# Short convolution and routed experts on one core: earlier halo loads, wider spacing of the expert batches, a bank of their own for the expert outputs, and counts summed in PSUM

## The chip, the cores and the metric

The kernel runs on one core of one Trainium2 chip. The metric is the device time of one execution in microseconds, as the median of several. The engines are called PE (TensorE, matmuls; PEld is its loading of weights), DVE (VectorE), ACT (ScalarE), POOL (GpSimd) and SP (SyncE, which here only issues DMAs). "SPq" or "POOLq" is the instruction sequencer of an engine.

## The reference

The input x has 8 sequences of 4160 rows with 192 numbers each. Each row is first replaced by a weighted sum of itself and the six rows before it, with seven softmax weights for each of eight heads of 24 numbers:

```
w = exp(weight_gen - max) ; w = w / (sum(w) + 1e-9)          # (B, S, 8 heads, 7 taps)
out[b, s, h, :] = sum over k of w[b, s, h, k] * x_pad[b, s + k, h, :]   # six zero rows ahead of each sequence
```

On that result, called y here, a gate picks 128 rows of every sequence, and only these go through a two-layer expert:

```
scores = y @ w_gate                                          # (B, S)
top_idx = the 128 rows of each sequence with the highest score
out[top_idx] = y[top_idx] + sigmoid(scores) * (relu(y[top_idx] @ w1) @ w2)   # 192 -> 1024 -> 192
```

All other rows of the output are y itself.

## The kernel before

**Layout.** The 33,280 rows are dealt to 128 partitions, 260 consecutive rows each, 16 partitions per sequence. Each partition needs the six rows ahead of its first row, the *halo*; for the first partition of a sequence they are zeros. x is read in chunks as float16 into a ring of `RING` = 168 row places (`xr`), by DMAs on POOL's queue (the type is changed on the way). A chunk is asked for when the ACT copy of a certain group of transposes begins, so POOL's loads follow the scoring, not the clock.

**Conv.** The loop runs over g = 0 to 65, four rows of every partition at a time, and each g has two halves. `products` (line 791) multiplies the seven shifted windows of x by the weights on DVE into a float16 tile (three tiles, `prodp`). `tap_sums` (line 801) adds the seven taps on PE with an identity matrix into a PSUM tile `cps`, one g later. `store` (line 809) copies it on ACT into one of three tiles `co`, and SP sends that to the output in two DMAs (line 811). A product covers all seven taps in one instruction (5376 numbers per partition) until the scores are complete; from then on, at g = 46, it is split in four and three taps, one part in each half (3072 and 2304 numbers).

**Weights.** weight_gen comes in 18 pieces on SP's queue (`load_wg`). For each, ACT makes the exponentials (line 643), PE sums the taps into the PSUM bank "den" (line 189), ACT turns the sum into its inverse by a logarithm and an exponential (lines 197 and 199), DVE multiplies (line 658), and ACT writes each weight twice (`dup_weights`, line 772) in the form that the products read.

**Scores.** They are found from x and not from y: `dots` transposes x on PE (line 719), ACT copies the transposes out (line 723), and PE multiplies them by a small matrix `gmat` that holds the gate vector, head by head (line 704, PSUM bank "yps"). `score` combines these with the weights. `gmat` is built on POOL with `affine_select` from four small loads of the gate vector (lines 106 to 119); those loads stand on SP's queue between the first piece of weights and the halo.

**The order of the work is written out by hand.** Every half of every g emits its product, then lets each of several generators do one step (`advance`), then emits the tap sums. A generator's step ends at `yield`. All engines therefore run their queues in this written order, and a wait of one instruction holds all that stands behind it on its engine. One advance of the generator `sel` happens per half once all scores are there, that is from g = 46: 40 advances while the conv loop lasts. After it, the `while` loop at line 917 goes on advancing `sel`, and after each advance emits the scatters that are ready.

**Selection** (`threshold_selection`). Each partition finds its 40 highest scores in five rounds of top 8. Four rounds then narrow a threshold for each sequence: DVE compares the 40 values with 23 thresholds (`above`, line 492, 920 results), sums the 40 results of each threshold (`cnt`, line 498), PE adds these over the 16 partitions of a sequence (`tot`, line 501), and DVE reads `tot` to move the threshold (lines 506 to 518). Then the row numbers are packed and a flag tells whether the list was too short; in that case a slow path after the loop does everything again. The value is read by all engines at line 929, after the loop.

**Experts** (`expert_pass`). For each of the eight sequences there is one batch of 128 rows. POOL gathers weights and windows of x by row number (lines 249 and 271). Ten steps follow, and the dictionary `steps` says how many advances after the start of its batch each is made; batches start `EVERY` = 3 advances apart, the first one `GWAIT` = 4 advances after the gathers were asked for:

```
0: row_weights, 1: scale_weights, 2: double, 3: tap_rows, 4: conv_rows,
5: turn_rows, 6: lambda b: hidden(b, 0), 7: lambda b: hidden(b, 1),
8: outputs, 9: hand_over,
```

`row_weights`: exponentials, tap sums and inverse on ACT, PE, ACT. `scale_weights`: two DVE products (lines 304 and 308). `double`: each weight written twice by ACT (`wes`, line 314). `tap_rows`: products of seven taps on DVE (line 320). `conv_rows`: tap sums on PE (`aps`, line 335) and two ACT copies. `turn_rows`: two transposes on PE (`tp`, line 347) and an ACT copy. `hidden`: half of the first layer on PE and a relu on ACT (line 369), twice. `outputs`: the second layer on PE (`yep`, line 377). `hand_over`: DVE scales by the gate value and adds the row (line 385). Inside one advance the steps of older batches come first. Of the eight PSUM banks, `cps` takes four, the transposes and the hidden layer share two ("tps"), and two single ones are "yps" and "den". Tap sums, `tp` and `yep` use "den"; `aps` and the selection's small results use "yps".

**End.** `scatter_rows` (line 417) writes the 128 rows of a batch over the conv's result, by an indirect DMA on POOL. It must come after all conv stores.

Of the kernel before, what the change touches and what calls it, by code (L numbers as in the profile page):

```python
# [20 lines left out]
def kernel(  # L21
# [22 lines left out]

    RING = 168
    C = 4
# [28 lines left out]

    nc.scalar.preload_act_table_set("natural_log_exp_and_others")

    scores = scp.tile([P, SP], FP32)
# [21 lines left out]

    wcol = scp.tile([P, 3], FP32)
    scrap = scp.tile([1, 1], FP32)

    def load_gate():
        wgv = moe_w_gate.rearrange("(d o) -> d o", o=1)
        nc.sync.dma_start(out=wcol[:, 0:1], in_=wgv[0:128, :])
        nc.sync.dma_start(out=wcol[0:64, 1:2], in_=wgv[128:192, :])
        nc.sync.dma_start(out=wcol[64:128, 1:2], in_=wgv[0:64, :])
        nc.sync.dma_start(out=wcol[:, 2:3], in_=wgv[64:192, :])

    def gate_matrix():
        gsel = scp.tile([P, 4, H], FP32)
        for j, (col, off) in enumerate(((0, 0), (1, 128), (1, -64), (2, 64))):
            nc.gpsimd.affine_select(
                out=gsel[:, j, :], in_=wcol[:, col:col + 1].to_broadcast([P, H]),
                pattern=[[-G, H]], compare_op=ALU.is_ge, fill=0.0,
                base=off, channel_multiplier=1,
            )
            nc.gpsimd.affine_select(
                out=gmat[:, j, :], in_=gsel[:, j, :],  # L120
                pattern=[[G, H]], compare_op=ALU.is_ge, fill=0.0,
                base=G - 1 - off, channel_multiplier=-1,
            )

    def selection_masks():
        nc.gpsimd.memset(ones32[:, :], 1.0)
# [75 lines left out]
    def expert_pass(rowf, gates, result, big):  # L202
# [92 lines left out]

        def row_weights(b):
            nc.scalar.activation(
                out=es[:, b, :, :],
                in_=wsel[:, b, :].rearrange("p (h k) -> p k h", k=K), func=AF.Exp
            )  # L300
            rws[b] = inverse(tap_sum(lambda k: es[:, b:b + 1, k, :], 1, H), 1, H)

# [28 lines left out]
        def conv_rows(b):  # L331
            mp = mp_of(b)
            aps = ps1.tile([P, D], FP32, tag="yps", name="aps")
            for k in range(K):
# [39 lines left out]
        def outputs(b):  # L374
            yep = ps1.tile([P, D], FP32, tag="den", name="yep")
            for j in range(FC):
# [15 lines left out]
        def hand_over(b):  # L392
# [3 lines left out]

        steps = {
            0: row_weights, 1: scale_weights, 2: double, 3: tap_rows, 4: conv_rows,
            5: turn_rows, 6: lambda b: hidden(b, 0), 7: lambda b: hidden(b, 1),
            8: outputs, 9: hand_over,  # L400
        }
        for _ in range(GWAIT):
            yield
        for t in range(EVERY * (B - 1) + 10):
            for off in sorted(steps, reverse=True):
# [29 lines left out]
    def threshold_selection():  # L435
# [49 lines left out]
        for r in range(ROUNDS):  # L485
# [18 lines left out]
            ge = scp.tile([P, NTHR], FP32, tag="ge", name="ge")  # L504
            nge = scp.tile([P, 1], FP32, tag="nge", name="nge")
            nc.vector.tensor_scalar(
                out=ge[:, :], in0=tot[:, :], scalar1=float(CAP) - 0.5, scalar2=None,
                op0=ALU.is_ge,
# [75 lines left out]
    def phase():  # L584
# [222 lines left out]
        def store(s, cps):  # L807
            co = outp.tile([P, 2, HB], FP32, tag="co", name="co")
            nc.scalar.copy(out=co[:, :, :], in_=cps[:, :, 0:HB])  # L809
            for j in range(2):  # L810
# [6 lines left out]
                )  # L817

        def selected():
            yield from threshold_selection()  # L820
# [5 lines left out]

        load_x(0, 4)
        load_wg(0)
        load_gate()
        make_identity(nc, identity[:])  # L830
        nc.vector.tensor_copy(out=ident16[:, :], in_=identity[:, :])
        halo = prodp.tile([P, PAD * D], FP32, tag="prod", name="halo")
        nc.vector.memset(halo[0:1, :], 0.0)
        for p0, p1 in ((1, Q), (Q, P)):
            nc.sync.dma_start(
                out=halo[p0:p1, :],
# [3 lines left out]
                ),  # L840
            )
        load_wg(1)
        load_x(4, 12)
        gate_matrix()
        selection_masks()
        load_wg(2)
        start_p = scp.tile([P, 1], FP32)
# [8 lines left out]
        for n in range(2):  # L856
# [3 lines left out]
            dup_weights(n)  # L860
            if n == 0:
                nc.vector.tensor_scalar(
                    out=xflat[:, 0:PAD * D], in0=halo[:, :],
# [12 lines left out]
        for g in range(NSUB + 1):  # L876
# [3 lines left out]
            for half in range(2):  # L880
# [28 lines left out]
            if g > 0:  # L909
                store(g - 1, cps)  # L910
            if g == 10:
                selection_constants()
# [16 lines left out]
    flag_v = nc.values_load(fast["flag"][0:1, 0:1], min_val=0, max_val=2 * P * B)  # L929
    with tc.If(flag_v > 0):  # L930
        with ExitStack() as fctx:
# [81 lines left out]
```

The softmax here doesn't subtract the row's maximum and nothing guards it: scores larger than these inputs give would overflow.

## Time and profile before

| | us |
|---|---|
| time, median of 3 (lowest, highest) | 317.03 (315.77, 319.07) |
| span of the profiled execution | 312.6 |
| DVE busy | 249.6 (80%) |
| PE busy | 194.0 (62%) |
| ACT busy | 188.9 (60%) |
| POOL busy | 56.5 (18%) |
| first conv product begins | 15.0 |
| first top-8 search (selection) begins | 182.9 |
| last eviction of a conv result begins | 288.3 |
| last scatter begins | 303.3 |

The page gives busy time over the whole span, and the kernel has stages with different limits, so the shares say little alone. Useful are the same numbers in stretches of the span, the list of who waited for whom, and the timeline around one step. A wait counts where its engine sets the pace of that stretch; the same wait on an engine with slack costs nothing.

### The profile page before, as it was taken

The page shows a single profiled execution, that of the slowest core. Times are in us where ns is not written, and L with a number is a line of the kernel's source. Part 1 is how long each engine was busy: PE and PEld are TensorE (multiplying, and loading weights), DVE is VectorE, ACT ScalarE, POOL GpSimd, SP SyncE. Part 2 cuts the span into 40 slices and gives each one's busy share as a digit, 9 for nine tenths or more (in the row PEclk, how much of TensorE's full clock was granted, in tenths as well). Part 3 has the DMA queues.
Part 4 walks back from the last instruction along what each step waited for, and adds up shares of the span by engine and source line. Part 5 has one row for each costly group of instructions (what it writes and reads, how often), then busy time and mean ns, then how long its engine had stood idle before and what let it go on. Part 6 is the DMA issues. An engine that isn't in the chain of part 4 may idle for free.

```text
span 312.6 us, 7490 instructions
## 1 busy us (share of the span) xinstructions
PE 194.0 (62%) x3177; PEld 123.2 (39%) x3177; DVE 249.6 (80%) x249; ACT 188.9 (60%) x282; POOL 56.5 (18%) x89
## 2 busy tenths in 40 slices
PE   0049778968697969698884850315727777778100
PEld 0026445635465636465552420103314454545000
DVE  2298995999989998999799999999997788882000
ACT  3279997899989979889684321111615557555100
POOL 3500000101010200101400000000348870000270
PEclk9999895989989779799799575555857999999755
DMA  7797999999999997999996331112467986233220
GB/s 96 221 242 226 219 249 241 193 240 271 260 256 228 257 253 150 214 216 206 229 221 181 102 103 51 50 42 60 74 183 122 175 195 145 55 100 101 72 77 13
DMA packets 29233, 51.50 MB, mean 165 GB/s; under 512 B 4933, under 2 KB 22603, under 8 KB 29194
## 3 DMA queue, kind: packets, MB, share of 16 engines
q0 software_dynamic: 7232, 17.34, 35.1%
q1 hardware_dynamic: 21962, 33.62, 34.3%
q8 instruction: 27, 0.44, 0.6%
q14 instruction: 12, 0.10, 0.1%
HBM read 41.60 MB, written 26.35 MB: 217 GB/s over the span
## 4 chain that ended last, share of the span: by engine, by line
DVE 27%; ACT 23%; PE 18%; DMA 17%; issue 8%; POOL 3%; SPq 2%; POOLq 0%; ACTq 0%; DVEq 0%
DVE prod L791 16%; DMA out_dram<-co 14%; PE cps L801 8%; ACT co L809 6%; ACT xT L723 5%; ACT e L643 4%; PE tps L719 3%; ACT wd L772 3%; DMA wg_t<-in_weight_gen_dram 3%; POOL out_dram L417 2%; PE den L189 2%; DVE above L492 1%; PE yps L704 1%; DVE cnt L498 1%; PE sps L750 1%
## 5 line engine op out<-in xcount | busy, mean ns | idle before, releaser
L791 DVE TENSOR_TENSOR prod<-xr,wd 128x5376 f16<-128x5376 f16 (+1 forms) x84 | 192.5, 2317 | 9.3 <-PE cps L801 5.5
L801 PE MATMUL cps<-prod,ident 64*64 64x384 f16 x1820 | 112.0, 375 | 9.0 <-DVE prod L791 8.9
L809 ACT COPY co<-cps 128x768 f32<-128x768 f32 x65 | 52.5, 808 | 47.8 <-PE cps L801 33.0
L801 PEld LDWEIGHTS <-ident 64*64 64x64 f16 x1820 | 49.9, 119 | 61.5 <-issue 26.4
L723 ACT COPY xT<-tps 128x1024 f16<-128x1024 f16 (+1 forms) x50 | 50.7, 1021 | 8.0 <-PE tps L719 7.7
L601 POOL DMA_DIRECT2D xr<-in_x_dram x28 | 15.1, 539 | 122.8 <-ACT xT L723 103.4
L719 PE MATMUL tps<-ident,xr 128*128 128x128 f16 x399 | 34.5, 236 | 2.4 <-DMA xr<-in_x_dram 2.4
L643 ACT ACTIVATE e<-wg_t 128x896 f16<-128x896 f32 (+2 forms) x18 | 30.0, 1666 | 8.0 <-DMA wg_t<-in_weight_gen_dram 8.0
L772 ACT COPY wd<-w 128x1792 f16<-128x1792 f16 (+2 forms) x18 | 28.0, 1554 | 0.8 <-DVE w L658 0.8
L189 PEld LDWEIGHTS <-ident 128*128 128x128 f16 x182 | 10.6, 104 | 43.3 <-issue 40.3
L719 PEld LDWEIGHTS <-xr 128*128 128x128 f16 x399 | 25.8, 105 | 2.9 <-DMA xr<-in_x_dram 2.6
L189 PE MATMUL den<-e,ident 128*128 128x128 f16 (+2 forms) x126 | 10.9, 235 | 24.2 <-ACT e L643 19.4
L704 PEld LDWEIGHTS <-xT 128*128 128x128 f16 x399 | 14.4, 98 | 23.8 <-issue 17.7
L704 PE MATMUL yps<-gmat,xT 128*128 128x8 f16 (+1 forms) x399 | 17.9, 169 | 9.0 <-ACT y L709 7.0
L249 POOL DMA_INDIRECT wsel<-in_weight_gen_dram,row_i x8 | 10.3, 1288 | 70.0 <-DVE win_i L217 67.9
L271 POOL DMA_INDIRECT xr<-in_x_dram,win_i x8 | 14.0, 1754 | 3.7 <-DVE xr L320 1.6
L417 POOL DMA_INDIRECT out_dram<-xr,row_i x8 | 7.8, 979 | 37.9 <-issue 37.9
L750 PE MATMUL sps<-sp,ident 128*128 128x256 f16 (+2 forms) x63 | 8.9, 290 | 7.8 <-ACT lnd L197 7.3
L501 PE MATMUL tot<-cnt,block 128*128 128x23 f16 x4 | 0.7, 178 | 19.1 <-DVE cnt L498 19.1
L369 ACT ACTIVATE hT<-hps 128x512 bf16<-128x512 f32 x16 | 9.5, 601 | 5.0 <-PE hps L365 5.0
L320 DVE TENSOR_TENSOR xr<-xr,wes 128x1344 f16<-128x1344 f16 x8 | 6.9, 857 | 6.8 <-ACT wes L314 6.8
L658 DVE TENSOR_TENSOR w<-e,r 128x896 f16<-128x896 f16 (+2 forms) x18 | 10.3, 572 | 2.2 <-ACT r L199 2.1
(126 smaller groups left out, 167.1 us busy)
## 6 DMA issues: line engine op xcount, KB each, us to landing
out_dram<-co SPq DMA_DIRECT2D x130, 192.0 KB, 5.2
xr<-in_x_dram POOLq DMA_DIRECT2D x22, 480.0 KB, 8.0
wg_t<-in_weight_gen_dram SPq DMA_DIRECT2D x15, 448.0 KB, 6.4
xr<-in_x_dram POOLq DMA_DIRECT2D x2, 576.0 KB, 8.0
halo<-in_x_dram SPq DMA_DIRECT2D x1, 504.0 KB
wg_t<-in_weight_gen_dram SPq DMA_DIRECT2D x2, 224.0 KB, 8.0
xr<-in_x_dram POOLq DMA_DIRECT2D x1, 384.0 KB, 7.0
w_sb<-in_moe_w_dram POOLq DMA_DIRECT2D x1, 384.0 KB
```

The lines of the kernel that those rows point to most:

```text
L189: nc.tensor.matmul(out=den[:, :, :], lhsT=ident16[:, :], rhs=e_k(k), start=(k == 0), stop=(k == K - 1),)
L271: nc.gpsimd.indirect_dma_start(out=win_of(b), out_offset=None, in_=x_elems, in_offset=bass.IndirectOffsetOnAxis(ap=win_i[:, b:b + 1], axis=0),
L417: ins = nc.gpsimd.indirect_dma_start(out=out_flat[:, :], out_offset=bass.IndirectOffsetOnAxis(ap=result["at"][:, b:b + 1], axis=0), in_=re ...
L601: return nc.gpsimd.dma_start(out=xr[:, o:o + b - a, :], in_=bass.AP(tensor=x_flat.tensor, offset=x_flat.offset + a * D, ap=[[SP * D, P], [ ...
L643: begun = nc.scalar.activation(out=es[n][:, :, :, :], in_=wgts[n].rearrange("p (s c) h k -> p s k (c h)", c=C), func=AF.Exp)
L704: nc.tensor.matmul(out=o, lhsT=lhs, rhs=m, start=(w == 0), stop=(w == 2), skip_group_check=True,)
L719: nc.tensor.transpose(out=tps[:, j, :], in_=xflat[:, e0:e0 + RUN], identity=ident16[:, :],)
L723: begun = nc.scalar.copy(out=xT[:, 0:m, :], in_=tps[:, 0:m, :])
L772: nc.scalar.copy(out=wd[:, 0:b - a, :, :, :], in_=w16[:, a:b, :, :, None].to_broadcast([P, b - a, K, CH, 2]),)
L791: nc.vector.tensor_tensor(out=pv[:, k0:k1], in0=xwin[:, k0:k1], in1=wv[:, k0:k1], op=MUL)
L801: nc.tensor.matmul(out=cps[64 * j:64 * j + 64, i, 0:HB], lhsT=ident16[rows, rows], rhs=pf[rows, k, j * HB:(j + 1) * HB], start=(k == 0), s ...
L809: nc.scalar.copy(out=co[:, :, :], in_=cps[:, :, 0:HB])
```

## The change

It has five parts.

1. *Start.* The two halo loads become the first instructions of ACT's queue, ahead of ACT's table load, and the larger one goes first. The four small loads of the gate vector move to ACT's queue, behind the first duplicated weights. The masks of the gate matrix are then made on POOL without the vector (`gate_masks`), and DVE multiplies the vector in after g = 1. The first three weight pieces stand together on SP's queue. This is to let the first product have its data earlier.
2. *Space.* The ring of x is shortened from 168 to 160 rows, and the room goes to a fourth `co` tile, so that an eviction need not wait for a store that is still under way.
3. *Counts.* The DVE sum over 40 results is gone. Five matmuls of 23 x 8 columns add the results over partitions and over five groups of the 40 in PSUM, and DVE sums the remaining 8.
4. *Spacing and bank.* `row_weights` is cut in two steps, the steps stand partly two advances apart, a batch lasts 13 advances and not 10, and batches start every 4 advances and not 3. The first starts one advance earlier. The last batches so come to lie past the conv loop. `yep` has the bank "yps", `aps` moves to "den". This is to take hand-overs between engines out of the way of the products.
5. *Flag.* All engines read the flag at g = 61 in the loop.

The diff, cut to its core:

```diff
-    RING = 168
+    RING = 160
...
-    nc.scalar.preload_act_table_set("natural_log_exp_and_others")
...
     def load_gate():
...
-        nc.sync.dma_start(out=wcol[:, 0:1], in_=wgv[0:128, :])
+        nc.scalar.dma_start(out=wcol[:, 0:1], in_=wgv[0:128, :])
...
+    def gate_matrix():
+        for j, (col, _) in enumerate(GATE_RUNS):
+            nc.vector.tensor_scalar(
+                out=gmat[:, j, :], in0=gsel[:, j, :], scalar1=wcol[:, col:col + 1],
+                scalar2=None, op0=MUL,
+            )
...
-        def row_weights(b):
+        def row_exps(b):
             nc.scalar.activation(
...
+        def row_sums(b):
             rws[b] = inverse(tap_sum(lambda k: es[:, b:b + 1, k, :], 1, H), 1, H)
...
-            aps = ps1.tile([P, D], FP32, tag="yps", name="aps")
+            aps = ps1.tile([P, D], FP32, tag="den", name="aps")
...
-            yep = ps1.tile([P, D], FP32, tag="den", name="yep")
+            yep = ps1.tile([P, D], FP32, tag="yps", name="yep")
...
-            0: row_weights, 1: scale_weights, 2: double, 3: tap_rows, 4: conv_rows,
-            5: turn_rows, 6: lambda b: hidden(b, 0), 7: lambda b: hidden(b, 1),
-            8: outputs, 9: hand_over,
+            0: row_exps, 1: row_sums, 3: scale_weights, 4: double, 6: tap_rows,
+            7: conv_rows, 8: turn_rows, 9: lambda b: hidden(b, 0),
+            10: lambda b: hidden(b, 1), 11: outputs, 12: hand_over,
...
-            above = scp.tile([P, NTHR, NLIST], BF16, tag="above", name="above")
+            above = scp.tile([P, NTHR, NLIST], FP16, tag="above", name="above")
...
-            cnt = scp.tile([P, NTHR], FP16, tag="cnt", name="cnt")
-            with nc.allow_low_precision("small counts are exact in fp16"):
-                nc.vector.tensor_reduce(out=cnt[:, :], in_=above[:, :, :], axis=AX.X, op=ADD)
             yield
-            tot = ps1.tile([P, NTHR], FP32, tag="yps", name="tot")
-            nc.tensor.matmul(
-                out=tot[:, :], lhsT=block16[:, :], rhs=cnt[:, :], start=True, stop=True
-            )
+            tot = ps1.tile([P, NTHR, 8], FP32, tag="yps", name="tot")
+            for c in range(0, NLIST, 8):
+                nc.tensor.matmul(
+                    out=tot[:, :, :], lhsT=block16[:, :], rhs=above[:, :, c:c + 8],
+                    start=(c == 0), stop=(c == NLIST - 8),
+                )
+            cnt = scp.tile([P, NTHR], FP32, tag="cnt", name="cnt")
+            nc.vector.tensor_reduce(out=cnt[:, :], in_=tot[:, :, :], axis=AX.X, op=ADD)
...
-        outp = cctx.enter_context(tc.tile_pool(name="outp", bufs=3))
+        outp = cctx.enter_context(tc.tile_pool(name="outp", bufs=4))
...
-        load_x(0, 4)
-        load_wg(0)
-        load_gate()
...
-        for p0, p1 in ((1, Q), (Q, P)):
-            nc.sync.dma_start(
+        for p0, p1 in ((Q, P), (1, Q)):
+            nc.scalar.dma_start(
                 out=halo[p0:p1, :],
...
+        nc.scalar.preload_act_table_set("natural_log_exp_and_others")
+        load_wg(0)
+        load_x(0, 4)
...
             if n == 0:
+                load_gate()
...
+                    if half == 1 and g == NSUB - 4:
+                        read_flag()
...
-    GWAIT = 4
-    EVERY = 3
+    GWAIT = 3
+    EVERY = 4
```

More of the change, by code (lines that the diff above doesn't have):

```diff
@@ L101 @@
     wcol = scp.tile([P, 3], FP32)
+    gsel = scp.tile([P, 4, H], FP32)
     scrap = scp.tile([1, 1], FP32)
@@ L105, in load_gate, with gate_masks @@
         wgv = moe_w_gate.rearrange("(d o) -> d o", o=1)
-        nc.sync.dma_start(out=wcol[:, 0:1], in_=wgv[0:128, :])
[L107 to L113, printed above, removed]
+        nc.scalar.dma_start(out=wcol[:, 0:1], in_=wgv[0:128, :])
+        nc.scalar.dma_start(out=wcol[0:64, 1:2], in_=wgv[128:192, :])
+        nc.scalar.dma_start(out=wcol[64:128, 1:2], in_=wgv[0:64, :])
+        nc.scalar.dma_start(out=wcol[:, 2:3], in_=wgv[64:192, :])
+    GATE_RUNS = ((0, 0), (1, 128), (1, -64), (2, 64))
+    def gate_masks():
+        nc.gpsimd.memset(ones32[:, :], 1.0)
+        for j, (_, off) in enumerate(GATE_RUNS):
             nc.gpsimd.affine_select(
-                out=gsel[:, j, :], in_=wcol[:, col:col + 1].to_broadcast([P, H]),
+                out=gsel[:, j, :], in_=ones32[:, 0:H],
                 pattern=[[-G, H]], compare_op=ALU.is_ge, fill=0.0,
@@ L119, in gate_matrix @@
             nc.gpsimd.affine_select(
-                out=gmat[:, j, :], in_=gsel[:, j, :],
+                out=gsel[:, j, :], in_=gsel[:, j, :],
                 pattern=[[G, H]], compare_op=ALU.is_ge, fill=0.0,
@@ L123, in gate_matrix @@
             )
+    def gate_matrix():
[4 more added lines that the diff above has]
+            )
     def selection_masks():
-        nc.gpsimd.memset(ones32[:, :], 1.0)
         bo = blockones.rearrange("p (b q) -> p b q", q=Q)
@@ L403, in expert_pass @@
             yield
-        for t in range(EVERY * (B - 1) + 10):
+        for t in range(EVERY * (B - 1) + max(steps) + 1):
             for off in sorted(steps, reverse=True):
@@ L506, in threshold_selection @@
             nc.vector.tensor_scalar(
-                out=ge[:, :], in0=tot[:, :], scalar1=float(CAP) - 0.5, scalar2=None,
+                out=ge[:, :], in0=cnt[:, :], scalar1=float(CAP) - 0.5, scalar2=None,
                 op0=ALU.is_ge,
@@ L817, in store, with read_flag @@
                 )
+        def read_flag():
+            fast["raised"] = nc.values_load(
+                fast["flag"][0:1, 0:1], min_val=0, max_val=2 * P * B
+            )
         def selected():
@@ L825, in selected @@
             fast["complete"] = True
-        load_x(0, 4)
-        load_wg(0)
-        load_gate()
-        make_identity(nc, identity[:])
-        nc.vector.tensor_copy(out=ident16[:, :], in_=identity[:, :])
         halo = prodp.tile([P, PAD * D], FP32, tag="prod", name="halo")
-        nc.vector.memset(halo[0:1, :], 0.0)
-        for p0, p1 in ((1, Q), (Q, P)):
-            nc.sync.dma_start(
+        for p0, p1 in ((Q, P), (1, Q)):
+            nc.scalar.dma_start(
                 out=halo[p0:p1, :],
@@ L841, in phase @@
             )
+        nc.scalar.preload_act_table_set("natural_log_exp_and_others")
+        load_wg(0)
+        load_x(0, 4)
+        make_identity(nc, identity[:])
+        nc.vector.tensor_copy(out=ident16[:, :], in_=identity[:, :])
+        nc.vector.memset(halo[0:1, :], 0.0)
         load_wg(1)
         load_x(4, 12)
-        gate_matrix()
+        load_wg(2)
+        gate_masks()
         selection_masks()
-        load_wg(2)
         start_p = scp.tile([P, 1], FP32)
@@ L910, in phase @@
                 store(g - 1, cps)
+            if g == 1:
+                gate_matrix()
             if g == 10:
@@ L928 @@
             phase()
-    flag_v = nc.values_load(fast["flag"][0:1, 0:1], min_val=0, max_val=2 * P * B)
-    with tc.If(flag_v > 0):
+    with tc.If(fast["raised"] > 0):
         with ExitStack() as fctx:
```

## The prediction

> **What bounds the kernel now.** I read the busy table first (VectorE, DVE below, 80% of the span, more than any other engine), then the busy time of every engine in six stretches that I cut at events of the timeline: first product, first top-8 search, first expert step, last product, last eviction. Columns: stretch, length, then busy us of PE, PEld, DVE, ACT, POOL, the granted PE clock, the DMA share and GB/s.
>
> ```profile
> 0.00:15.00 15.00, 0.88 (x14) 0.79 (x15) 2.86 (x8) 4.36 (x8) 6.30 (x26) 1.00 0.74 154
> 15.00:182.90 167.90, 131.42 (x2249) 84.44 (x2248) 155.58 (x92) 140.13 (x175) 16.40 (x31) 0.89 0.92 220
> 182.90:230.00 47.10, 19.29 (x265) 10.12 (x266) 45.44 (x100) 10.03 (x16) 2.89 (x3) 0.58 0.30 74
> 230.00:281.70 51.70, 34.61 (x534) 22.82 (x534) 43.73 (x50) 29.29 (x73) 22.46 (x15) 0.92 0.62 130
> 281.70:288.40 6.70, 5.88 (x94) 3.77 (x94) 1.54 (x3) 3.32 (x9) 0.00 (x0) 1.00 0.45 117
> 288.40:312.60 24.20, 1.88 (x24) 1.27 (x21) 0.42 (x1) 1.73 (x3) 8.43 (x15) 0.59 0.18 52
> ```
>
> From 15 to 281.7 us DVE is the pace: idle 12.3 of 167.9, 1.7 of 47.1, 8.0 of 51.7. Before 15 us nothing computes; after 281.7 DVE is out of it. So I price DVE time up to the last product, then the two tails. DVE's waits (total, times, longest):
>
> ```profile
> DVE xr L862 <- DMA halo<-in_x_dram: 7.4, 1, 7.4
> DVE xr L320 <- ACT wes L314: 6.8, 7, 1.1
> DVE xr L385 <- PE yep L377: 6.6, 2, 3.4
> DVE prod L791 <- PE cps L801: 5.5, 6, 2.3
> ```
>
> The second row recurs once per expert batch. The timeline of one batch shows its cause (start, duration, and in brackets the idle time before it with what ended it):
>
> ```profile
> 253.30 0.41 DVE L385 SCALAR_TENSOR_TENSOR xr<-yep,gate,xr 128x192 f32<-128x192 f32 x1
> 253.76 0.27 PE L347 MATMUL tp<-ident_bf,xeb 128*128 128x128 bf16 x2 [0.96 <-DVE xr L385]
> ...
> 254.07 0.37 ACT L352 COPY xeT<-tp 128x256 bf16<-128x256 bf16 x1 [1.19 <-PE tp L347]
> 254.34 0.29 ACT L314 COPY wes<-we 128x112 f16<-128x112 f16 x1
> 254.66 0.86 DVE L320 TENSOR_TENSOR xr<-xr,wes 128x1344 f16<-128x1344 f16 x1 [0.95 <-ACT wes L314]
> ```
>
> The output product yep and the transposes tp share the one "den" bank. PE may not write tp before DVE's L385 has read yep, ACT's wes copy stands behind the copy of tp, and DVE's next instruction needs wes. It is a ring of four hand-overs, 0.95 us of DVE each time.
>
> The start, from the chain of waits and the timeline:
>
> ```profile
> 3.62 0.86 SPq L835 DMA_DIRECT2D halo<-in_x_dram  x2
> 12.48 1.01 ACT L643 ACTIVATE e<-wg_t 128x448 f16<-128x448 f32 x1 [7.13 <-DMA wg_t<-in_weight_gen_dram]
> 14.96 5.82 DVE L791 TENSOR_TENSOR prod<-xr,wd 128x5376 f16<-128x5376 f16 x2
> ```
>
> Halo and second weight piece stand behind four small gate loads on SP's queue and land at 12.1 and 12.5; the first product follows 2.5 us later. The end, from the chain:
>
> ```profile
> 289.81 3.45 DMA out_dram<-co
> ...
> 294.34 1.01 POOL out_dram L417
> ...
> 303.34 0.97 POOL out_dram L417
> ```
>
> Eight scatters at 1.28 us each wait for the last conv store; 8.3 us follow the last one.
>
> **What the Trainium skill says.** "DMA: Bandwidth & Descriptors", section "Issuing engines are not separate DMA queues": DMAs of scalar, sync and gpsimd run on the same 16 engines and interleave, so another queue saves issue time only. The trace agrees in part: 0.42 to 0.59 us per issue on SP, but 8 us from issue to landing for the piece behind. "PSUM — Partial Sum Buffer", section "Engine vs sequencer instructions": ScalarE, VectorE and GpSimdE queues are strict FIFO; wes above shows it. "VectorE: DVE Perf Modes", section "The perf-mode tier table (the rule you actually need)": tensor_reduce has only the 1x mode; here 920 elements took 1.114 us. "TensorE: Matmul & The Clock Gate", section "What's actually happening": activity releases the clock throttle; the granted clock is 0.58 in the selection stage with PE 41% busy, 0.92 in the expert stage with 67%.
>
> **Part by part.** *Start.* Halo goes out on ACT's queue before the table load, weight pieces lose the gate loads ahead of them. ACT: two issues (0.49 and 0.33 on SP) and the 1.28 us table load from 0.82 end near 3.0, so the first exponential stays near 3.0, wd ends near 5.4. Then the four gate issues (2.2 us on SP) hold ACT to about 7.7. Behind them is the second exponential; product needs it plus the 2.5 us measured, so 10.2 at best. Do halo and piece land by then? Over 8 to 13 us the DMA moved some 280 GB/s. Halo 0.57, pieces 0 and 1 0.34, first x rows 0.39 MB read, together 1.3 MB, plus a like share of the next x rows and pieces: about 2.0 MB from 2 us at 220 to 280 is 9 to 11 us. I take the first product at 10.8: -4.2 (range -2 to -5). Removing the gate masks' wait from POOL costs nothing: POOL's next load waits for ACT's exponential anyway. *Gate product on DVE*: four small tensor_scalars at about 0.12 (the small ones of the constants follow each other at 0.08 to 0.15): +0.5. They now wait for the gate loads, and the third conv product is queued behind them; but issued by 7.7 and landing 2.1 to 7.0 us later, those are there by 15, and the gate product comes up only after two products, near 16.5. *Fourth co buffer*: ACT waited 4.1 us for stores in the conv stage; DVE idles 12.3 there, of which 5.5 for PE's cps behind such evictions. A third of that: -1.5 (0 to -3). *RING 160*: x loads run some six dot groups ahead, and a slot overwritten was last read about 5 groups of four rows before; no wait, 0.
>
> *Counts.* Each of 4 rounds loses the 1.03 us that cnt takes from start to next start. PE adds five matmuls of 184 columns; seven of 256 took 0.93 to 1.09 at clocks near 0.9, so 0.5 to 1.2 us with the lower clock, behind the 1.26 to 1.67 us product which DVE runs in between: nothing. On PE only tap sums of products already made are queued behind these matmuls, and their eviction has slack (ACT is 10.0 of 47.1 us busy). DVE adds a reduce of 184 elements from PSUM: between 0.16 (16 elements, PSUM) and 0.40 (256, SBUF); I take 0.35, +0.05 for the dependence. (1.03 - 0.40) x 4: -2.5.
>
> *Expert stage up to the last product.* Waits of 5.8 (wes) and 1.9 (L304 for r) before 281.7. With yep in the other bank PE's transposes no longer wait for DVE, and one or two half-steps (1.3 to 1.75 us of products each) now lie between producer and consumer, so both go. But four half-steps per batch bring PE 2 x 1.52 of tap sums and 3.5 of expert matmuls, 6.5 us in a period of 4 x 1.465 + 1.55 = 7.4: 88%. I leave 2.0 us of waits: -5.7 (-3 to -7.7). The order lets fewer steps fall inside: counting advances (one per half-step; steps start one earlier, spaced four), by the last product the kernel now runs 8 weight scalings, 7 tap products, 5 finishes, afterwards 6, 5 and 4. 2 x 0.40 (0.18 and 0.22) + 2 x 0.78 (start to next start) + 0.37: -2.7. Flag read: 0.61 us on DVE's sequencer, which ran ahead of a busy POOL in this trace; on PE it took 1.04. Behind it on DVE stands the next product: between 0 and 1, I take +0.3. At the end it gains nothing, since POOL's own read fell beside a scatter.
>
> *Last product to last eviction*, 6.7 us: PE waits there for L385 and carries hidden layers, taps and outputs of two batches. Afterwards two tap-sum halves (0.84, 0.68), one hidden half (0.66), one yep (0.83), one aps (0.74), 3.7, with hand-overs 4.0: -2.7 (-1.5 to -3.5).
>
> *Tail.* The store lands 4.9 us after the eviction starts and the eighth scatter begins 15.0 after it. Five batches are ready at once, three finish during the train. Their chain from the eviction on, by measured durations (turn 0.3, copy 0.4, hidden 0.7 twice, relu 0.6, yep 0.9, aps 0.7, copy 0.35, hand-overs 0.05 to 0.4): about 4.7 for batch 5, 5.1 each for 6 and 7: 14.9. The two end together: +0.5 (-0.3 to +4).
>
> Sum: -4.2 + 0.5 - 1.5 - 2.5 - 5.7 - 2.7 + 0.3 - 2.7 + 0.5 = -18.0 on 317.0: 299.0 us.
>
> **Rivals.** *A, the DMA takes the start back.* For: its share is 0.92 over the conv stage and near 1.0 from 30 to 120, stores land after about 10 us, and the chain passes through them for 14% of the span. Against: ACT waited for them only 4.1 us. Start and buffer then give 1.5 in place of 5.7: 303.2. *B, PE and ACT become the bound* of the denser expert stage, or the three batches past the conv outlast the scatters. For: 88% of PE. Against: more activity kept the clock at 1.0. Then 2 more us of waits and 4 of tail: 305. *C, slower.* Thirteen half-steps past the conv have no product to hide behind. If each costs 2.0 us (a PE matmul group and an ACT pass, 0.7 + 0.6, with hand-overs), they take 26 in place of 15, and if also start, buffer and waits give nothing, there is -2.5 - 2.7 + 11 + 0.8 = +6.6: 323.6. Against: neighbouring steps belong to different batches and overlap.
>
> **How the numbers follow.** Forecast 0.62, A 0.16, B 0.13, C 0.05, and 0.04 that gains and losses cancel. 299.0 is the likeliest case. With the ends of the terms above, all good gives about 292, A and B together about 309; 293 to 308 leaves out C and the outer ends. Faster 0.89, same 0.04, slower 0.07.
>
> **What would show it.** First product near 10.8; no wait of L862 beyond 3 us; no reduce of 920 elements and one from tot near 0.35; no PE wait of tp for L385 and no L320 wait for wes of 0.9; last product near 266, last eviction near 270; scatters without gaps from about 276, the last begun 15 to 16 us after the eviction. Wrong would be: PE or ACT continuously busy in the expert stage, gaps before the last scatters, a longer wait for stores in the conv stage.

## The result and the profile after

The changed kernel takes 286.79 us (median of 4, 285.44 to 289.6), beside 316.4 us (315.49 to 319.07) for the kernel before on the same chip: ratio 0.9063, 95% interval 0.8974 to 0.9152. The forecast was 299.0, with 308 and 293 as its ends. A run more than 1.5% above the fastest run of its kernel counts as slow; medians here are over all runs, ratios over the others. The direction is as forecast, and the time lies 12 us below the forecast.

First the busy times after, in four of the six stretches shown before, cut at the same events (columns: stretch, length, busy us of PE, PEld, DVE, ACT, POOL, PE clock, DMA share, GB/s).

```profile
0.00:11.56 11.56, 0.88 (x14) 0.79 (x15) 2.79 (x8) 4.36 (x8) 5.65 (x26) 1.00 0.79 199
11.56:172.89 161.33, 124.35 (x2249) 80.94 (x2248) 155.67 (x97) 139.68 (x175) 15.87 (x30) 0.94 0.94 229
...
217.50:257.70 40.20, 31.75 (x487) 20.07 (x483) 39.56 (x45) 23.57 (x58) 22.25 (x15) 0.85 0.75 169
...
261.40:284.90 23.50, 8.25 (x99) 6.23 (x98) 3.38 (x7) 6.99 (x19) 8.40 (x15) 0.84 0.20 59
```

The second row is the surprise: DVE does the same work (155.67 us, 155.58 before) in 161.33 us in place of 167.90. Its idle time fell from 12.3 to 5.7 us. For the account I cut the trace of each kernel at seven events. "Row numbers" is the first packing of row numbers, where the selection has ended and the experts begin. The last column is what the prediction's terms say for that stage.

| stage | before | after | difference | forecast |
|---|---|---|---|---|
| start, to the first product | 14.96 | 11.56 | -3.4 | -4.2 |
| conv, to the first top-8 search | 167.94 | 161.33 | -6.6 | -1.0 |
| selection, to the row numbers | 36.32 | 33.25 | -3.1 | -2.5 |
| experts, to the end of the last product | 62.42 | 51.58 | -10.8 | -8.1 |
| last product to last eviction | 6.70 | 3.67 | -3.0 | -2.7 |
| last eviction to last scatter | 15.00 | 14.27 | -0.7 | +0.5 |
| last scatter to the end | 9.26 | 9.24 | 0.0 | 0 |
| span | 312.6 | 284.9 | -27.7 | -18.0 |

So the stages explain 9.7 us of the miss, 5.6 of them in the conv stage. The other 2.5 us come from the execution: the profile of before was taken from one of 314.31 us while the forecast started from the median of 317.03. Part of them may lie in the expert stage, whose length is not steady with the old spacing: 62.4 us in the kernel before, and 63.6, 64.3 and 64.5 us in three kernels below that keep the order of this stage (new start with buffer, buffer, shorter ring). With the new spacing it is 51.1 to 51.6 us in all eleven profiles, so the 10.8 us of the table are the low end of that gain.

DVE's wait for tap sums in the conv stage, first of the kernel before, then of the changed one (total, times, longest):

```profile
DVE prod L791 <- PE cps L801: 5.5, 6, 2.3
```

```profile
DVE prod L801 <- PE cps L811: 2.1, 2, 1.7
```

Behind ACT's copies for the scores (ss) DVE waited 4.1 us in all before and waits 1.1 us after.

In the expert stage up to the last product, the list had two rows before, and that of the changed kernel has a single one:

```profile
DVE xr L320 <- ACT wes L314: 5.8, 6, 1.1
DVE we L304 <- ACT r L199: 1.9, 5, 0.6
```

```profile
DVE prod L801 <- PE tp L356: 0.4, 1, 0.4
```

The timeline around one step shows the ring of four hand-overs gone. The transposes of one batch start at 232.78, while the yep of the next older batch is still unread in the other bank (DVE reads it at 233.58), and wes of the next younger batch is ready 2.8 us before DVE's L329 comes to it:

```profile
232.78 0.27 PE L356 MATMUL tp<-ident_bf,xeb 128*128 128x128 bf16 x2
...
233.58 0.41 DVE L394 SCALAR_TENSOR_TENSOR xr<-yep,gate,xr 128x192 f32<-128x192 f32 x1
...
233.77 0.30 ACT L323 COPY wes<-we 128x112 f16<-128x112 f16 x1
...
236.84 0.85 DVE L329 TENSOR_TENSOR xr<-xr,wes 128x1344 f16<-128x1344 f16 x1
```

The start, from the timeline of ACT with the first product of DVE:

```profile
0.83 1.12 ACTq L844 DMA_DIRECT2D halo<-in_x_dram  x2
...
5.00 0.60 ACT L653 ACTIVATE e<-wg_t 128x224 f16<-128x224 f32 x1 [1.73 <-DMA wg_t<-in_weight_gen_dram]
...
9.08 1.00 ACT L653 ACTIVATE e<-wg_t 128x448 f16<-128x448 f32 x1 [1.68 <-issue]
...
11.56 5.82 DVE L801 TENSOR_TENSOR prod<-xr,wd 128x5376 f16<-128x5376 f16 x2
```

No wait of the halo is left. The second exponential now stands behind ACT's own issues of the gate loads ("<-issue"), and the product follows it by 2.48 us as it did before.

The sum of one selection round after:

```profile
186.44 0.34 DVE L513 TENSOR_REDUCE cnt<-tot 128x23 f32<-128x184 f32 x1
```

The reduce of 920 is gone, the one from PSUM takes 0.34 us, and DVE does not wait for PE's five matmuls (0.92 us), which run beside the product.

### The profile page after: what moved, and what is told of

It reads as the page before. It is cut to its first block, busy times and chain, and to the rows that moved or that the text cites. A ratio compares the mean times of both kernels' runs of the same rounds, so it can differ in the third digit from the quotient of the medians.

```text
span 284.9 us, 7530 instructions
## 1 busy us (share of the span) xinstructions
PE 191.8 (67%) x3193; PEld 123.1 (43%) x3193; DVE 245.9 (86%) x253; ACT 187.5 (66%) x282; POOL 55.1 (19%) x88
## 5 line engine op out<-in xcount | busy, mean ns | idle before, releaser
L811 PE MATMUL cps<-prod,ident 64*64 64x384 f16 x1820 | 108.9, 369 | 10.2 <-DVE prod L801 10.0
L811 PEld LDWEIGHTS <-ident 64*64 64x64 f16 x1820 | 49.1, 117 | 42.2 <-DVE prod L801 13.4
L611 POOL DMA_DIRECT2D xr<-in_x_dram x27 | 14.5, 539 | 116.3 <-ACT xT L733 93.1
L729 PE MATMUL tps<-ident,xr 128*128 128x128 f16 x399 | 33.2, 230 | 1.4 <-DMA xr<-in_x_dram 1.4
L729 PEld LDWEIGHTS <-xr 128*128 128x128 f16 x399 | 24.7, 102 | 2.3 <-DMA xr<-in_x_dram 1.7
L256 POOL DMA_INDIRECT wsel<-in_weight_gen_dram,row_i x8 | 11.9, 1488 | 70.1 <-DVE win_i L224 67.9
L508 PE MATMUL tot<-above,block 128*128 128x184 f16 x20 | 3.7, 349 | 13.9 <-DVE above L501 13.9
L278 POOL DMA_INDIRECT xr<-in_x_dram,win_i x8 | 11.8, 1475 | 5.6 <-DVE xr L329 4.1
L760 PE MATMUL sps<-sp,ident 128*128 128x256 f16 (+2 forms) x63 | 7.7, 263 | 6.2 <-ACT lnd L204 6.2
L370 PE MATMUL hps<-xeT,w_a 128*128 128x128 bf16 x64 | 8.9, 223 | 2.3 <-ACT xeT L361 1.8
```

The costliest lines, as they stand in the source:

```text
L256: nc.gpsimd.indirect_dma_start(out=wsel[:, b, :], out_offset=None, in_=wg_flat[:, :], in_offset=bass.IndirectOffsetOnAxis(ap=row_i[:, b:b ...
L278: nc.gpsimd.indirect_dma_start(out=win_of(b), out_offset=None, in_=x_elems, in_offset=bass.IndirectOffsetOnAxis(ap=win_i[:, b:b + 1], axis=0),
L611: return nc.gpsimd.dma_start(out=xr[:, o:o + b - a, :], in_=bass.AP(tensor=x_flat.tensor, offset=x_flat.offset + a * D, ap=[[SP * D, P], [ ...
L729: nc.tensor.transpose(out=tps[:, j, :], in_=xflat[:, e0:e0 + RUN], identity=ident16[:, :],)
L811: nc.tensor.matmul(out=cps[64 * j:64 * j + 64, i, 0:HB], lhsT=ident16[rows, rows], rhs=pf[rows, k, j * HB:(j + 1) * HB], start=(k == 0), s ...
```

## The experiments

Times are medians, ratios are to the kernel before on the same chip, in brackets the 95% interval. "Idle" is DVE's idle time in the conv stage.

**The parts alone, put into the kernel before.** The buffer:

```diff
-    RING = 168
+    RING = 160
-        outp = ... tile_pool(name="outp", bufs=3)
+        outp = ... tile_pool(name="outp", bufs=4)
```

> The kernel before with the fourth co tile and the ring of 160 rows alone. Theory 1 (the fourth tile took the idle time out of the conv stage): DVE idles 5 to 7 us less between its first product and the first top-8 search (before: 12.3 us), about 311 us in all. Theory 2 (the other start did it, by what stands in the queues): idle stays near 12, under 1.5 us gained, 315 to 317.

It took 310.41 us, ratio 0.9833 [0.9746, 0.9921]. Its conv stage (columns as above):

```profile
15.23:177.55 162.32, 128.32 (x2249) 83.45 (x2248) 155.36 (x93) 140.01 (x175) 15.88 (x30) 0.91 0.94 229
```

Idle is 7.0 us and the stage 162.32, against 12.3 and 167.94: nearly the whole gain of the conv stage comes from these two lines. The shorter ring without the fourth tile, in a single run, brought none of it (317.55 us, idle 13.8):

> The kernel before with the ring of 160 rows alone, three co tiles. Theory 1 (the tile and not the ring): conv stage idle 10 to 15 us, as in the six profiles with three tiles, store throughput near 225 GB/s from 20 to 150 us. Rival (the ring): idle near 6.

The new start (order of the loads, gate loads on ACT, gate product on DVE), alone and together with the buffer:

> The kernel before with the new start alone (halo on ACT's queue, gate loads behind the first doubled weights, gate product on DVE). First product near 11.6 us, as in the changed kernel, so 3.4 us earlier. Theory 1: the conv stage keeps its 12 us of DVE idle time, total gain 3 to 3.5, about 313. Theory 2: its idle time falls to about 6 as well, total gain 9 to 10, about 307.

> The kernel before with the new start and with the ring of 160 and four co tiles, nothing else. Theory 1 (the two work only together): first product 11.6, conv stage idle about 6, gain 9 to 10, about 307. Rival (they add up as measured alone, 5.5 for the tile and 0 to 3 for the start): 308 to 311.

Alone it took 315.9 us as the median of four runs that lie far apart (310.99 to 318.87); the ratio, 0.9885 [0.9765, 1.0004], rests on the lower two and does not exclude no change. Together it took 306.82 us, 0.9694 [0.9601, 0.9787]. With four tiles the gain is kept in full: against the buffer alone the first product begins at 11.52 in place of 15.23 and the conv stage is as long (162.30 and 162.32 us). Whether three tiles would give part of it back, as rival A has it, stays open: the conv stage of the three-tile kernel with the early start below is 169.78 us, those of four three-tile kernels with the old start 165.6 to 169.3 us.

The counts in PSUM:

> The kernel before with the counts summed in PSUM alone. From the first top-8 search to the row numbers 33.3 us in place of 36.3, so 3.1 gained there, and the rest unchanged: about 313.5. Rival (PE's matmuls hold DVE): a wait of the reduce for tot appears, gain under 1.5.

314.54 us, 0.9919 [0.9885, 0.9953]. The selection stage takes 33.3 us in every profile with the counts in PSUM and 36.3 us in every one without.

The banks exchanged, with nothing else:

```diff
-            aps = ps1.tile([P, D], FP32, tag="yps", name="aps")
+            aps = ps1.tile([P, D], FP32, tag="den", name="aps")
-            yep = ps1.tile([P, D], FP32, tag="den", name="yep")
+            yep = ps1.tile([P, D], FP32, tag="yps", name="yep")
```

> The kernel before with yep and aps exchanged between the two PSUM banks alone, batches still three advances apart. Theory 1 (the shared bank made the wait of tap_rows for wes): those six waits of 0.95 us go, the waits of L304 for r (1.9 us in all) stay, and the time from the last product to the last eviction falls too; gain 6 to 9, about 309. Rival (the short spacing made them): waits stay, gain under 2.

The spacing, with nothing else (the diff's new `steps`, `row_exps` and `row_sums`, EVERY 4, GWAIT 3; yep still shares its bank with tp), and both together:

> The kernel before with the new steps and spacing alone, yep still in the bank of tp and the tap sums. Theory 1 (bank): PE still waits for DVE before tp, but with a step between double and tap_rows DVE no longer stands for it; the moved work alone gives 2.7 and the waits that go 5 to 8: gain 7 to 11, about 307. Rival (both needed): waits of about 1 us per batch stay on DVE, gain near 4, about 312; and the three batches past the conv, chained through DVE, end later than the scatters, so that the tail grows by up to 4.

> The kernel before with bank and spacing together. Theory: DVE idle from the row numbers to the last product under 1.5 us (spacing alone 0.6), last product to last eviction 2.4 to 3.7 in place of 6.0 with spacing alone, 14.3 to 14.8 from there to the last scatter if PE's signals for the last hidden layer come in time, 17.7 if they come late as in three of the profiles. In all 300 to 304. Rival (the bank adds nothing to the spacing): 305.

Bank 309.76 us, 0.9827 [0.9739, 0.9915]; spacing 305.34, 0.9661 [0.9578, 0.9743]; both 304.34, 0.9624 [0.9492, 0.9756]. The waits of DVE in the expert stage, first with the bank alone (its two longest rows), then with the spacing alone:

```profile
DVE xr L320 <- ACT wes L314: 1.9, 3, 1.2
DVE we L304 <- ACT lnd L197: 1.5, 1, 1.5
...
```

```profile
DVE we L306 <- ACT r L199: 0.8, 2, 0.6
```

The spacing removes the waits, and it does so with the shared bank: DVE idles 0.5 us in the expert stage, 8.2 before. The bank alone thins them out, from 5.8 to 1.9 us for wes, but 6.2 us of idle time stay in a stage of 60.27 us, beside 51.34 with the spacing and 51.1 with both. My theory that the bank makes the wait was half right: it takes the bank and steps that fall into one advance. What the bank adds lies behind the last product: from there to the last eviction it is 6.71 us before, 4.91 with the bank alone, 6.02 with the spacing alone and 2.41 with both. In the profile of the spacing alone the PE clock fell to 0.5 for 3.4 us just there, so part of the 3.6 us between the last two may be the clock's. The times of the two (305.34 and 304.34) don't tell them apart.

All parts but the early flag read:

> The changed kernel with the flag read after the loop, as in the kernel before. Theory: the read costs and gives nothing, since it runs beside other work in both places: within 1 us of 287. Rival (the read in the loop pays at the end, or costs each engine up to 1 us): 1 us or more off, either way.

290.83 us, 0.919 [0.9097, 0.9282]. Its profiled span is 4.4 us longer than that of the changed kernel, but 3.4 of that is a gap before the last scatter, taken up below, which also stands in kernels with the early read. Its expert stage is 51.34 us against 51.58 (51.57 to 51.63 in the eight profiles with the early read). So the early flag read costs about 0.24 us there, near the 0.3 forecast; what it gains at the end can't be read from this, and the expected 287 us, give or take one, did not come.

**How many store tiles.** Taken from the changed kernel, by the number in `bufs` alone (3, then 2 in a single run); five tiles needed the ring cut to 152 rows. In that last kernel the working space of the experts overlies some rows of x that later products still need, so it computes those rows from other data; its instructions and transfers are the same.

> The changed kernel with three co tiles in place of four, ring still 160. Theory 1 (the fourth tile makes the earlier start hold, and without it the stores give the start back): DVE idle in the conv stage goes from 5.7 to 11 to 15 us, first product stays at 11.6, total 6 to 9 above the changed kernel, about 294. Rival (the other edits took the idle time out, or the shorter ring did): within 2 us of 287.

> The changed kernel with two co tiles. Theory 1 (stores in flight set the rate of the conv stage): idle well above the 13 us of three tiles, 25 to 50 us, with ACT waiting for stores for most of it and a DMA rate below 220 GB/s, though the DMA's share of busy time stays above 0.85. Rival (the tile only took away single collisions, as the prediction held): idle up by another 2 to 4 us.

> The changed kernel with five co tiles and a ring of 152 rows. Theory S (stores in flight limit the conv stage: 29, 13 and 6 us of DVE idle with 2, 3 and 4 tiles): 3 to 5 us idle with five, DMA above 243 GB/s, ACT waits for stores under 2 us, 284 to 286 us if the end is as in the changed kernel. Rival R (four are enough, or the shorter ring makes x come late): 6 us or more idle, 286.8 us or above, and a wait of the product for x if the ring is the cause.

Three tiles: 297.55 us, 0.9376 [0.9267, 0.9486]. Two: 315.01 us. Five: 290.51 us, 0.9235 [0.911, 0.9361]. The conv stage of each, columns as above, with two, three and five tiles (four is the second row after):

```profile
11.50:197.20 185.70, 135.42 (x2249) 86.59 (x2248) 156.37 (x96) 140.04 (x175) 15.93 (x30) 0.87 0.85 199
```

```profile
11.54:181.32 169.78, 130.85 (x2249) 84.74 (x2248) 156.43 (x96) 139.70 (x175) 15.87 (x30) 0.89 0.91 218
```

```profile
11.64:175.80 164.16, 126.72 (x2249) 82.20 (x2248) 155.98 (x96) 139.80 (x175) 15.87 (x30) 0.93 0.94 226
```

DVE's work is the same in all, 156 us; its idle time is 29.3, 13.4, 5.7 and 8.2 us. ACT's wait for stores in that stage is 27.0, 11.4, 4.3 and 1.2 us; the rows of two and of five:

```profile
ACT co L819 <- DMA out_dram<-co: 27.0, 15, 4.5
```

```profile
ACT co L819 <- DMA out_dram<-co: 1.2, 2, 0.9
```

The wait shrinks with each tile, but from four to five nothing more comes through to DVE; the theory that stores still limit the stage with four tiles falls. (Five tiles came with a shorter ring, but no wait of DVE or PE for x appears.) That five are worse than four is not shown by the idle time: the changed kernel profiled a second time has 7.1 us. Over all profiles, idle is 10 to 15 us with three tiles and 5.7 to 7.5 with four. The three-tile kernels differ in ACT's wait for stores (4.1 us in the kernel before, 6.8 with the shorter ring, 11.4 here) far more than in DVE's idle time (12.3, 13.8, 13.4), so that row alone does not measure the loss. It is not even steady in one program: up to the selection the kernel with the spacing alone is the kernel before, yet it has 9.3 us at 11.8 idle (kernel before first, then that one):

```profile
ACT co L809 <- DMA out_dram<-co: 4.1, 6, 1.5
```

```profile
ACT co L811 <- DMA out_dram<-co: 9.3, 9, 1.8
```

How the loss gets to DVE shows best with two tiles:

```profile
DVE prod L801 <- ACT wd L782: 10.0, 4, 5.6
DVE prod L801 <- PE cps L811: 9.7, 5, 3.2
DVE sp L753 <- ACT y L719: 5.0, 4, 1.8
```

A late store holds one ACT eviction, and ACT works through its queue in the written order. So the duplicated weights (wd), the copies for the scores (y, ss) and the evictions that free cps all come late, and DVE meets each of them under another name.

Was the DMA the limit in the conv stage of before? Its share was 0.98 from 50 to 80 us. The same stretch with only the buffer added (before first, then the buffer kernel):

```profile
50.00:80.00 30.00, 25.75 (x462) 16.84 (x459) 26.26 (x25) 25.81 (x32) 2.64 (x5) 0.88 0.98 235
```

```profile
50.00:80.00 30.00, 23.80 (x449) 15.96 (x448) 29.06 (x26) 28.84 (x37) 3.17 (x6) 0.94 1.03 274
```

At nearly the same share it moved 274 GB/s in place of 235, so a share of 0.98 does not mean that 235 GB/s was its limit.

**The start and the tail.** The gate loads back on SP's queue, behind the third weight piece:

```diff
-        nc.scalar.dma_start(out=wcol[:, 0:1], in_=wgv[0:128, :])     # and three more
+        nc.sync.dma_start(out=wcol[:, 0:1], in_=wgv[0:128, :])       # and three more
```

> The changed kernel with the four gate loads on SP's queue behind the third weight piece, in place of ACT's queue behind the first doubled weights. Theory (the 2.2 us of gate issues on ACT hold back the second exponential, whose data is there): the second exponential begins at about 7.4 in place of 9.1, the first product near 9.9, total 1.0 to 1.7 less, about 285.5. Rival (the weight piece or the halo lands no earlier, or the conv stage waits it back): no change, 286 to 287.5.

```profile
7.44 1.00 ACT L653 ACTIVATE e<-wg_t 128x448 f16<-128x448 f32 x1
```

The second exponential begins at 7.44 in place of 9.08 and the first product at 9.91 in place of 11.56: the four issues on ACT cost 1.65 us. The last product ends 1.2 us earlier than in the changed kernel, and the last eviction, at 258.97, comes 2.4 us earlier. Yet the time is 289.84 us, 0.9154 [0.9067, 0.9242]. In the profile (of its fastest run, 287.74 us) the gain is lost again in the last batch (ACT of this kernel, then its last scatter):

```profile
271.51 0.60 ACT L378 ACTIVATE hT<-hps 128x512 bf16<-128x512 f32 x1 [2.41 <-PE hps L374]
274.35 0.60 ACT L378 ACTIVATE hT<-hps 128x512 bf16<-128x512 f32 x1 [2.24 <-remote]
```

```profile
276.63 0.97 POOL L426 DMA_INDIRECT out_dram<-xr,row_i  x1 [3.60 <-DVEq L949]
```

PE's matmuls of both hidden halves are recorded between 269.16 and 270.2, but ACT gets their signals at 271.5 and 274.3. In the changed kernel the two relus run back to back, and its scatters have no gap:

```profile
271.97 1.09 ACT L378 ACTIVATE hT<-hps 128x512 bf16<-128x512 f32 x2 [0.76 <-PE hps L374]
```

The seven kernels with the new spacing so far fall in two groups: 17.6 to 17.7 us from the last eviction to the last scatter in six, 14.27 in the changed kernel. Two theories on the gap: that it depends on where PE is in its stream of instructions (40 unused small matmuls on PE early in the start shift that place), or on the single execution:

> The changed kernel once more, unaltered. Theory P (PE's place in its instruction stream decides whether the signals of the last batch's hidden layer come late): it comes at 285 to 287 us again, the last scatter begins 14 to 15 us after the last eviction and without a gap before it. Rival T (chance of an execution decides): the profile may show the gap of 3.4 us, 17.6 us from eviction to last scatter, and the runs fall in two groups, near 286 and near 289.5.

> The changed kernel with 40 small matmuls added in PE's empty time at the start, whose result nothing reads; they shift PE's later instructions by 80 places and take none of its paced time. Theory P: the place of the late signals moves, so either the last product to last eviction falls from 3.7 to 2.4 us and the time to some 285, or the gap of 3.4 us appears ahead of the last scatter and the time is some 289. Rival T: same 14.3 us and 286.8 as the changed kernel.

> The changed kernel with the four gate loads on SP's queue behind the third weight piece, and the same 40 matmuls added at the start. Theory P: the gap before the last scatter goes, 14 to 15 us from the last eviction to the last scatter, and the start's 1.65 us show: 284 to 286.5 us, faster than the changed kernel. Rival T: 17.6 us stays, and 289.8 us as without the matmuls.

The unchanged kernel again: 287.48 us (287.26 to 289.18), 14.30 us, no gap; the five-tile kernel has none either. With 40 matmuls it took 289.29 us, and the version with the gate loads on SP 288.71 us (287.61 to 290.55). Both of these have no gap before the last scatter; instead the first scatter begins 6.7 and 6.8 us after the last eviction (5.2 to 5.3 in the others) and the last one 15.7 and 15.8 after it. Whether that is the same delay in another place is not shown, and the expected 284 to 286.5 us did not come. The recorded ends of matmuls are modelled, so the records can't say what PE did in between. Two things the trace does tell. In the kernel shown above, with the loads on SP, no packet of instructions moves from 268.9 to 275.3 us, so the delay does not end with an instruction fetch that lands late. And in all six kernels with the gap the PE clock falls to 0.5 within this batch (at 272.8 us in the one shown), in the five profiles without it only after the batch (at 277.5 in the changed kernel). Here the first relu begins at 271.51, already late, so the delay starts before the recorded fall, which may be its result. Why those signals come late stays open, and so does whether an execution of the changed kernel can have the gap (one in four of its runs takes 289 us, but none of those was profiled). No version tried here beats the changed kernel.

## Why the prediction was wrong

**The step that failed** is the fourth buffer: "ACT waited 4.1 us for stores in the conv stage; DVE idles 12.3 there, of which 5.5 for PE's cps behind such evictions. A third of that: -1.5 (0 to -3)". The mechanism was right, the size was not: -5.4 us of idle time in the kernel with the buffer alone, -6.6 of stage in the full change, twice the outer end. The mistake was to price a wait by the row that carries its name. A late store showed up in DVE's list as waits for PE, for weights and for scores. With the buffer alone the row itself went only from 4.1 to 3.4 us, and 4.1 was a low draw beside the 9.3 above. The better bound was the 12.3 us of idle time itself, most of it waits for results of ACT and of PE, which is served by ACT. This term is the largest part of the miss: with the conv stage right, the forecast would have been 293.4 us. The rest is 2.7 us in the expert stage, 2.5 us between the profiled execution and the median, and smaller terms.

**Start**: -3.4 against -4.2. "The first exponential stays near 3.0" was wrong: it came at 5.0 (2.9 before). Its weight piece is now issued at the same moment as the halo, whose 0.58 MB move from 2 to 5 us; that this holds the piece back is likely, but no run shows it. The chain behind it held: gate issues, then the second exponential, then 2.48 us to the product (2.5 forecast). The Trainium skill's page "DMA: Bandwidth & Descriptors", section "Issuing engines are not separate DMA queues", says both halves of this: the transfers share the engines whoever issues them, and another queue saves only the issue time, "which is usually small". Here four issues of 0.36 to 0.60 us on a computing engine were not small: 1.65 us on the path. **Gate product**: +0.5, measured 0.62.

**Counts**: -3.1 against -2.5, the reduce at 0.34 us as forecast; the gain per round was 0.77 us, since the sum had also had to wait for `above` (1.15 us from start to start), where the product now follows it after 1.03. **Experts**: -10.8 against -8.1; of it -7.4 are idle time (-5.7 forecast) and -3.5 work (-2.4 with the flag read). The numbers of steps inside the stage came out as forecast (6 scalings, 5 tap products and an edge of the sixth, 4 finishes). The 2.0 us of waits that I left because PE would be busy 88% did not come; 0.4 did, though PE is busy 79% (31.75 of 40.20 us). The first half of rival B falls: its waits are absent. Its second half, batches that outlast the scatters, holds for six kernels with the new spacing, though not for the changed one. The argument against it, that more activity keeps the clock at 1.0, failed: the PE clock in this stage was 0.90 before, 0.84 after and 0.96 in the second profile. But the stage took 51.58 and 51.62 us at these last two, so its length did not follow the clock. **Last product to last eviction**: -3.0 against -2.7, right with luck. The second profile has 2.41 us in place of 3.67, which is -4.3 and outside the range given. All three profiles with 3.7 us have a clock of 0.5 for 3.4 us until 0.7 us before the last product ends; the six with 2.41 have 1.0 throughout. **Tail**: -0.7 against +0.5, just outside its range: right about batches that finish during the train of scatters, with the reservation that six other kernels with the new spacing showed 3.4 us more there.

**Rival A** had the DMA as the limit, because its share was over 0.9. The 274 GB/s above speak against it, and "stores land after about 10 us" was misread: the median in that stage is 6.1 us, and only the longest pass 10. The Trainium skill's page "Perfetto Trace Analysis", section "Identifying the Most-Contended Engine", warns that occupancy of the 16 DMA engines misleads and that the use of the memory bandwidth should be read in its place. For occupancy this case agrees, with shares of 0.91, 0.94 and 0.94 for three, four and five tiles at idle times of 13.4, 5.7 and 8.2 us.

## What to carry to other kernels

When a buffer is added to an engine that serves several others in order, bound the gain by the idle time of the engine that sets the pace, not by the wait rows that name the buffer; then find the right number of buffers by stepping it (here two, three, four and five: 29, 13, 6 and 8 us idle). The wait that recurred once per batch was a ring of hand-overs: spreading the steps broke it, splitting the shared bank alone only thinned it out, and doing both paid little more. Keep DMA issues off the queue of an engine whose next instruction is on the path.

## What was not expected of the hardware

The busy share of the DMA hardly tells what it moves: 235 GB/s at 0.98 and 274 GB/s at 1.03 in the same stretch of two kernels. PE's signal that a group of matmuls is done reached ACT up to 4 us after the recorded matmuls in the last batch of six kernels with the new spacing; the cause stays open. And two profiles of the same program differ by 1.5 us of DVE idle time in the conv stage and by 1.3 us between last product and last eviction, the latter with a PE clock that fell to 0.5 for 3.4 us in one of them; so one profile can't settle a smaller difference.
